# Reordering the weight conversion, the fetches and the pacing of a kernel's first 160 microseconds

## The chip, the cores and the metric

The kernel runs on one core of a Trainium2 chip. The metric is the device time of one execution in microseconds, and medians are given over repeated runs. Kernels that are compared in one experiment ran on the same chip beside runs of the kernel before, whose median there was 1023.8 to 1025.1 us.

## The reference

```python
# attention: q, k, v are (8, 8, 576, 64)
scores = q @ k.transpose(0, 1, 3, 2) / sqrt(64)
ret = scores * Dmat                   # gamma[h] ** (i - j) for i >= j, else 0
x = (ret @ v)                         # laid out as 4608 tokens of 512
# feed-forward with squared ReLU; w_in (512, 2048), w_out (2048, 512)
h = np.maximum(x @ w_in, 0.0)
out = (h * h) @ w_out
```

The weights come as 64-bit floats, and the core has to turn them into 32-bit floats itself.

## The kernel before

The work comes in three interleaved streams.

- **Retention**, 40 chunks of up to 128 tokens. TensorE makes scores, VectorE multiplies them by a mask (`ret`), TensorE transposes the next chunk's k and q (`turn`), ScalarE copies kT, and VectorE makes qT. `retain_a`, `_b` and `_c` add up the chunk's x.
- **Conversion** of w_in in 16 pieces of 128 x 512. Each piece takes five VectorE operations and two of ScalarE. `convert(n)` issues the next n parts of a list.
- **Block 0** of the feed-forward, 16 steps, one for each piece of w_in. Step j needs piece j finished. Later blocks of 28 steps follow.

Python emits everything in one order (the schedule is manual), and where the traces were read for it, ScalarE and VectorE took their share in that order: in the trace of this kernel the transposes for kT of one chunk ended at 25.95 us, and ScalarE's copy of kT began at 27.41, behind three conversion operations begun at 25.61, 26.24 and 26.80. So the place at which a part is issued among the other streams decides what it stands behind.

```python
def round_parts(j):                       # piece j; cut
    def one():
        nc.vector.tensor_scalar(exp, hi, 20, 0x7FF, ...)                 # L205
        nc.scalar.activation(exp, exp, AF.Relu, bias=..., scale=...)     # L207
    def two():
        nc.vector.tensor_scalar(bits, hi, 0xFFFFF, 0x100000, ...)        # L211
        nc.scalar.activation(frac, lo, AF.Copy, scale=2.0 ** -52)        # L212
    def three():
        nc.vector.scalar_tensor_tensor(t, bits, 2.0 ** -20, frac, ...)   # L215
    def four():
        nc.vector.tensor_tensor(t, t, exp, op=ALU.mult)                  # L218
    def five():
        nc.vector.scalar_tensor_tensor(bits, hi, 0x80000000, bits, ...)  # L221
    ...

def w_in_parts():                         # the list that convert() goes through
    end = []
    for j in range(N_W1 + 1):
        one, two, three, four, five = round_parts(j) ...
        yield from (one, two) if j < N_W1 else ()
        yield from end                    # three, four, five of piece j - 1
        ...

def first_in(j):                          # step j of block 0; cut
    assert n_made[0] > j
    for c in range(N_DM):
        nc.tensor.matmul(p, lhsT=w[:, c, :], rhs=xT[0][:, c, :], ...)    # L528, h_ps

R_0 = TOK * 3 // 2                        # tokens of retention beside block 0

def ffn(i):                               # cut: pays out steps at a rate per token
    rate = (N_W1 - 2) / R_0 if tok >= TOK else 0
    owed[0] += cs / 3 * rate
    while steps and owed[0] >= 1:
        owed[0] -= 1
        if steps[0][0] == 0:
            convert(4)
        step()

for i in range(N_CH + 1):                 # cut
    if i <= N_EARLY:                      # N_EARLY = 4
        ...retain_a, _b, _c of i - 1, with idle matmuls: warm(n)
        if i == N_EARLY: step()
        scores(i)
        warm(2)
        convert(3 if i >= 2 else 0)
        if i == N_EARLY: step()
        turn(i + 1)
        warm(1)
        convert(2 if i >= 2 else 0)
    else:
        retain_a(i - 1); convert(1); ffn(i - 1)
        retain_b(i - 1); scores(i); convert(1); ffn(i - 1)
        turn(i + 1); retain_c(i - 1); convert(1); ffn(i - 1)
    load(i + 3) ...; fetch_raw(...)       # next chunk's q, k, v; next raw pieces
```

Of the kernel before, what the change touches and what calls it, by code (L numbers as in the profile page):

```python
# [12 lines left out]
AF = mybir.ActivationFunctionType  # L13
# [4 lines left out]
TOK = 512  # L18
# [22 lines left out]
def kernel(  # L41
# [33 lines left out]
    nc = tc.nc  # L75
# [79 lines left out]
    N_W1 = N_DF  # L155
# [7 lines left out]
    def raw_of(j):  # L163
        return raw_all[j % N_RAW] if j < N_W1 else raw_all[(j - N_W1) % 3]

    def exp_of(j):
        return exp_all[j % 2] if j < N_W1 else exp_all[2 * (j % 2)]

    def piece_src(j):
        wi, m, e = pieces[j]  # L170
        f = (m + e * N_M) * 128
        if wi == 0:
            return moe_w_in.rearrange("(c p) f -> p c f", p=128)[:, :, f:f + 128]
        return moe_w_out[f:f + 128, :].rearrange("p (c f) -> p c f", c=N_DM)
# [8 lines left out]
    def as_dst(j, t):  # L183

        if pieces[j][0] == 0:
            return t.rearrange("p (c f) -> p c f", c=N_DM)
        return t.rearrange("p (o s f) -> p o s f", o=2, s=2)
# [7 lines left out]

    def round_parts(j):
        words = raw_of(j).bitcast(U32).rearrange("p (n two) -> p n two", two=2)
        lo, hi = words[:, :, 0], words[:, :, 1]
        frac = raw_of(j).rearrange("p (n two) -> p n two", two=2)[:, :, 0]
        exp = exp_of(j).bitcast(U32)  # L200
        t = piece_dst(j)
        bits = t.bitcast(U32)

        def one():
            nc.vector.tensor_scalar(exp, hi, 20, 0x7FF, op0=ALU.logical_shift_right, op1=ALU.bitwise_and)  # L205

            nc.scalar.activation(exp, exp, AF.Relu, bias=exp_bias[:, 0:1], scale=2.0 ** 23)  # L207

        def two():

            nc.vector.tensor_scalar(bits, as_dst(j, hi), 0xFFFFF, 0x100000, op0=ALU.bitwise_and, op1=ALU.bitwise_or)  # L211
            nc.scalar.activation(frac, lo, AF.Copy, scale=2.0 ** -52)  # L212

        def three():
            nc.vector.scalar_tensor_tensor(t, bits, 2.0 ** -20, as_dst(j, frac), op0=ALU.mult, op1=ALU.add)  # L215

        def four():
            nc.vector.tensor_tensor(t, t, as_dst(j, exp_of(j)), op=ALU.mult)  # L218

        def five():  # L220
            nc.vector.scalar_tensor_tensor(bits, as_dst(j, hi), 0x80000000, bits, op0=ALU.bitwise_and, op1=ALU.bitwise_or)  # L221

        if not wide:
            to = t if pieces[j][0] == 0 else t.rearrange("p o s f -> p (o s) f")
            return [lambda: nc.sync.dma_start(to, piece_src(j))] + [None] * 4
        return [one, two, three, four, five]

    def sum_w_in(mp):

# [13 lines left out]
    def w_out_parts():  # L243

        for j in range(N_W1, N_W1 + 3):
            yield lambda j=j: fetch_w(j)
        for j in range(N_W1, len(pieces)):
            *most, five = round_parts(j)
            yield from most

            def last(j=j, five=five):
                if five:
                    five()
                fetch_w(j + 3)

            yield last
            wi, m, e = pieces[j]
            mh, mq = divmod(m, N_MQ)
            if e == 1:

                at = slice(2 * mh, 2 * mh + 2)
                b = [stage[0][:, o, at, :] for o in range(4)] + [stage[1][:, o, at, :] for o in range(3)]
                r1, r2, r3, r4 = right_sums(*b)
                yield lambda r1=r1, r2=r2: (r1(), r2())
                yield lambda r3=r3, r4=r4: (r3(), r4())
            if e == 1 and mh == 1:

                for st_, at in ((stage[0], slice(0, 4)), (stage[1], slice(4, 7))):
                    yield from right_sums(*(st_[:, :, o, :] for o in range(NP)))
                    yield lambda st_=st_, at=at, mq=mq: nc.sync.dma_start(  # L270
                        w2_dram[at, :, mq, :].rearrange("o p f -> p o f"), st_.rearrange("p o s f -> p o (s f)"))
# [4 lines left out]
    def fetch_raw(count):  # L276

        for _ in range(count):
            if n_raw[0] < min(N_W1, n_made[0] + N_RAW):
                fetch_w(n_raw[0])  # L280
                n_raw[0] += 1


    def w_in_parts():

        end = []
        for j in range(N_W1 + 1):
            one, two, three, four, five = round_parts(j) if j < N_W1 else [None] * 5
            yield from (one, two) if j < N_W1 else ()
            yield from end  # L290

            def last(j=j, five=five):
                if five:
                    five()
                n_made[0] += 1
                if n_next[0]:
                    fetch_raw(2)

            end = [three, four, last]

    w_in_steps = w_in_parts()

    def convert(count):
        for _ in range(count):
            f = next(w_in_steps, None)
            f and f()
# [3 lines left out]
    exp_bias = const.tile([128, 1], F32, name="exp_bias")  # L310
    nc.gpsimd.memset(exp_bias, -896.0 * 2.0 ** 23)
    for i in range(3):
        load(i)
        fetch_raw(min(i, 1))

    ident = only.tile([128, 128], F32, name="ident")
    make_identity(nc, ident)
# [95 lines left out]
    def grown(i, h):  # L413
        nc.scalar.copy(u_sb[(2 * chunks[i][1] + h + 1) % 3], u_ps[0])
# [28 lines left out]
    def retain_c(i):  # L443

        b_, ci, c0, cs = chunks[i]
        own, grow = within(i, 0)
        more = ci + 1 < NCH
        if i < N_EARLY or i >= N_CH - 2:

            nc.scalar.copy(u_sb[(2 * ci + (cs // CH)) % 3][:, 0:2, 0:1], xp[0][:, :, cs - CH:cs - CH + 1])  # L450
        for j in range(0, len(own), 2):
            for f in own[j:j + 2] + (grow[j:j + 2] if more else []):
                f()
        if more:
            grown(i, 1)
        tok = b_ * S + c0
        at = tok
        p = xp[0][:, :, 0:256].rearrange("p a (g t) -> p a g t", g=2)
        while at < tok + cs:
            n = at // TOK  # L460

            while steps and steps[0][0] <= (n - 2 if n > 4 else n - 3):
                step()
                owed[0] -= 1
            end = min(tok + cs, (n + 1) * TOK)
            nc.scalar.copy(xT[n][:, :, at - n * TOK:end - n * TOK].rearrange("p (a g) t -> p a g t", a=2),  # L466
                           p[:, :, :, at - tok:end - tok])
            at = end
            if n_next[0] < N_BLK and (n_next[0] + 1) * TOK <= at:
                steps.extend(block_steps(n_next[0]))  # L470
                n_next[0] += 1
        st[i] = loaded[i] = None
# [154 lines left out]



    R_0 = TOK * 3 // 2  # L630
    LAG = 7

    def ffn(i):

        b, ci, c0, cs = chunks[max(0, min(i, N_CH - 1))]
        tok = b * S + c0
        if tok < TOK + R_0:
            rate = (N_W1 - 2) / R_0 if tok >= TOK else 0
        elif tok < 5 * TOK:
            rate = (3 * N_MP * NP - LAG) / (4 * TOK - TOK - R_0 + TOK)  # L640
        else:
            rate = N_MP * NP / TOK
        owed[0] += cs / 3 * rate
        while steps and owed[0] >= 1:
            owed[0] -= 1
            if steps[0][0] == 0:
                convert(4)
            step()


# [2 lines left out]
    def warm(count):  # L653
        for _ in range(count):
            nc.tensor.matmul(junk[:, 0:128], lhsT=ident, rhs=ident, start=True, stop=True)
# [4 lines left out]
    for i in range(N_CH + 1):  # L660
        if i <= N_EARLY:

            if i >= 1:
                retain_a(i - 1)
                warm(1)
                retain_b(i - 1)
                warm(1)
                retain_c(i - 1)
            if i == N_EARLY:
                step()  # L670
            scores(i)
            warm(2)
            convert(3 if i >= 2 else 0)
            if i == N_EARLY:
                step()
            turn(i + 1)
            warm(1)
            convert(2 if i >= 2 else 0)
        else:
            retain_a(i - 1)  # L680
            convert(1)
            ffn(i - 1)
            retain_b(i - 1)
            if i < N_CH:
                scores(i)
            convert(1)
            ffn(i - 1)
            if i + 1 < N_CH:
                turn(i + 1)
            retain_c(i - 1)  # L690
            convert(1)
            ffn(i - 1)
        if i + 3 < N_CH:
            load(i + 3)
        if i < N_EARLY:
            fetch_raw(1 if i < 2 else 2)
    assert n_next[0] == N_BLK
    first.close()

# [207 lines left out]
```

## Time and profile before

| | before |
|---|---|
| median of runs | 1024.22 us |
| profiled span, granted clock | 1024.3 us, 0.989 |
| TensorE idle in the whole span | 32.2 us, of it 19.3 us up to 160 us |
| step 0 of block 0 starts | 40.64 us |
| busy from 40 to 137 us | TensorE 90%, VectorE 67% |

TensorE sets the time (it is busy for 992.1 of 1024.3 us), so the reader should ask of each engine only when it makes TensorE wait. The change aims at one line of the waits of ScalarE up to 137 us (who waited <- for whom: us in total, times, longest):

```profile
ACT w L207 <- DVE w L205: 34.2, 14, 4.2
```

When L207 stood and waited for L205 in this trace, the copies of kT, u_sb and x stood behind it, and for those TensorE did wait: L207 began at 83.79 us after a wait of 3.41 us, the three copies followed at 84.90, 85.37 and 85.63, and TensorE waited 1.16 us for x, to 86.34. Its waits for u_sb are 5.9 us in all.

### The profile page before, as it was taken

Reading aid. Unit: us, or ns where it says so; the run is one execution under the profiler, and the core shown is the slowest. Engines: PE = TensorE matmul, PEld = TensorE weight load, DVE = VectorE, ACT = ScalarE, POOL = GpSimd, SP = SyncE. Lnnn points to the kernel's source line nnn. Section 1 sums busy time; section 2 is a strip of 40 time slices with the busy share of each in tenths; the row PEclk is TensorE's granted clock in tenths of the full one; section 3 lists DMA queues with packets and bytes.
Section 4 is the critical chain, followed back from the end, with each engine's and each line's share of the span. In section 5 each row is a group of like instructions: output and inputs, shape, how many; then the busy total and the mean of one; then the engine's idle time right before and its main releaser. Section 6 shows DMA issues by size and latency. Waiting matters only on the chain.

```text
span 1024.3 us, 24209 instructions
## 1 busy us (share of the span) xinstructions
PE 992.1 (97%) x10442; PEld 867.8 (85%) x10442; DVE 748.3 (73%) x1414; ACT 184.1 (18%) x425; POOL 79.6 (8%) x82
## 2 busy tenths in 40 slices
PE   7788999999999999999999999999999999999998
PEld 6444578888888888888778888999999999999997
DVE  1367858765888897898886767877777677777765
ACT  2344331121222212222221100000000000000000
POOL 1100101011011010210101000000000000000000
PEclk9899999999999999999999999999999999999999
DMA  8758556565668759769537898874855747565351
GB/s 204 192 149 232 129 150 208 144 191 166 165 232 260 219 192 288 232 184 301 185 108 280 325 414 322 310 263 170 276 200 214 275 155 252 200 240 206 124 206 42
DMA packets 187659, 220.36 MB, mean 215 GB/s; under 512 B 119200, under 2 KB 137632, under 8 KB 178592
## 3 DMA queue, kind: packets, MB, share of 16 engines
q1 hardware_dynamic: 187552, 218.81, 65.0%
q8 instruction: 82, 1.34, 0.5%
q14 instruction: 25, 0.20, 0.1%
HBM read 129.39 MB, written 89.39 MB: 214 GB/s over the span
## 4 chain that ended last, share of the span: by engine, by line
PE 87%; DVE 6%; DMA 3%; ACT 2%; SPq 1%; issue 1%; DVEq 0%; ACTq 0%
PE o_b L787 16%; PE h_b L563 15%; PE o_c L787 11%; PE o_a L787 10%; PE h_c L563 10%; PE h_a L563 10%; PE h_ps L528 5%; PE x_ps L405 3%; PE t_ps L367 2%; PE x_ps L440 2%; PE sc_ps L388 2%; DMA g_dram<-room 1%; DMA a<-g_dram 1%; PE u_ps L408 1%; DVE ret L391 1%
## 5 line engine op out<-in xcount | busy, mean ns | idle before, releaser
L563 PE MATMUL h_b<-room,w 128*128 128x256 f32 x736 | 177.6, 384 | 1.4 <-DVE room L582 1.4
L563 PEld LDWEIGHTS h_b<-room,w 128*128 128x128 f32 x736 | 136.9, 190 | 21.6 <-DVE room L582 2.2
L787 PE MATMUL o_b<-w,room 128*128 128x128 f32 x1168 | 144.5, 275 | 1.4 <-DVE room L738 1.4
L787 PEld LDWEIGHTS o_b<-w,room 128*128 128x128 f32 x1168 | 137.2, 192 | 1.6 <-DVE room L738 1.6
L787 PE MATMUL o_c<-w,room 128*128 128x128 f32 x1008 | 123.0, 275 | 0.0
L787 PEld LDWEIGHTS o_c<-w,room 128*128 128x128 f32 x1008 | 117.7, 192 | 0.0
L563 PE MATMUL h_c<-room,w 128*128 128x256 f32 x480 | 115.8, 384 | 0.0
L563 PE MATMUL h_a<-room,w 128*128 128x256 f32 x448 | 107.5, 383 | 0.0
L563 PEld LDWEIGHTS h_c<-room,w 128*128 128x128 f32 x480 | 89.3, 190 | 12.8
L563 PEld LDWEIGHTS h_a<-room,w 128*128 128x128 f32 x448 | 83.8, 190 | 12.3 <-issue 0.5
L787 PE MATMUL o_a<-w,a 128*128 128x128 f32 x688 | 85.9, 275 | 0.5 <-DMA a<-g_dram 0.5
L787 PEld LDWEIGHTS o_a<-w,a 128*128 128x128 f32 x688 | 81.3, 192 | 0.7 <-issue 0.6
L570 DVE SCALAR_TENSOR_TENSOR room<-room 128x512 f32<-128x512 f32 x96 | 70.7, 736 | 3.3
L580 POOL TENSOR_TENSOR room<-room 128x512 f32<-128x512 f32 x32 | 35.7, 1115 | 441.0 <-ACT room L579 398.0
L528 PE MATMUL h_ps<-room,w 128*128 128x512 f32 x128 | 65.2, 657 | 2.5 <-DVE w L221 1.5
L798 ACT COPY r<-o_a 128x128 f32<-128x128 f32 x54 | 14.4, 266 | 278.4 <-PE o_a L787 237.3
L375 DVE TENSOR_TENSOR qT<-t_ps,dq 128x512 f32<-128x512 f32 (+1 forms) x40 | 25.4, 634 | 44.2 <-ACT kT L373 33.7
L405 PEld LDWEIGHTS x_ps<-ret,v_ld 64*64 64x64 f32 x1152 | 40.2, 137 | 19.0 <-issue 14.5
L582 DVE TENSOR_TENSOR room<-h_b,room 128x512 f32<-128x512 f32 x32 | 22.1, 691 | 44.9 <-PE h_b L563 40.6
L405 PE MATMUL x_ps<-ret,v_ld 64*64 64x64 f32 x1152 | 50.1, 227 | 4.8 <-ACT w L466 1.6
L393 POOL TENSOR_TENSOR v_ld<-v_ld,dv 128x512 f32<-128x512 f32 (+1 forms) x40 | 43.7, 1094 | 98.0 <-DMA v_ld<-in_v_dram 91.0
L528 PEld LDWEIGHTS h_ps<-room,w 128*128 128x128 f32 x128 | 25.1, 206 | 30.7 <-issue 26.8
(95 smaller groups left out, 1364.6 us busy)
## 6 DMA issues: line engine op xcount, KB each, us to landing
g_dram<-room SPq DMA_DIRECT2D x32, 1792.0 KB, 7.2
a<-g_dram SPq DMA_DIRECT2D x43, 1024.0 KB, 6.8
room<-g_dram SPq DMA_DIRECT2D x20, 1024.0 KB, 5.9
w<-w_dram SPq DMA_DIRECT2D x7, 1792.0 KB, 11.1
out_dram<-room SPq DMA_DIRECT2D x18, 512.0 KB, 3.3
v_ld<-in_v_dram SPq DMA_DIRECT2D x32, 256.0 KB, 3.9
w<-in_moe_w_in_dram SPq DMA_DIRECT2D x16, 512.0 KB, 4.9
w<-in_moe_w_out_dram SPq DMA_DIRECT2D x16, 512.0 KB, 3.8
```

What stands on the lines that cost most here:

```text
L367: nc.tensor.transpose(p[:, h, j, hp, :], loaded[i][j][rows(h), 2 * hp:2 * hp + 2, :], ident[rows(h), rows(h)])
L375: nc.vector.tensor_tensor(to, p[:, :n_h, j, :, :], dq[:, :, c0:c0 + cs].rearrange("p d (h t) -> p h d t", h=n_h), op=ALU.mult)
L388: nc.tensor.matmul(sc[rows(h), e, hp, :], lhsT=kT[rows(e), hp, t], rhs=qT[rows(e), hp, t], start=True, stop=True, skip_group_check=True)
L393: nc.gpsimd.tensor_tensor(vs[:cs], vs[:cs], dv[:cs, :, ci:ci + 1].to_broadcast([cs, H, D]), op=ALU.mult)
L405: own.append(lambda hp=hp, e=e, b=b: nc.tensor.matmul(x_at(hp, b, h), lhsT=s["vs"][rows(h), 2 * hp + b, :], rhs=s["ret"][rows(h), e, hp, : ...
L440: nc.tensor.matmul(x_at(hp, b, h), lhsT=u[rows(e), hp, :], rhs=s["qT"][rows(e), hp, CH * h:CH * h + CH], start=clears(b, hp // 2), stop=Fa ...
L528: nc.tensor.matmul(p.rearrange("p h t -> p (h t)"), lhsT=w[:, c, :], rhs=xT[0][:, c, :], start=(c == 0), stop=(c == N_DM - 1))
L563: nc.tensor.matmul(p[:, mm, :], lhsT=w[:, c, :], rhs=xs[n][right][:, c, :], start=(j in OPENS and mm == 0 and c == 0), stop=(j in CLOSES a ...
L570: nc.vector.scalar_tensor_tensor(t, t, 0.0, t, op0=ALU.max, op1=ALU.mult)
L580: nc.gpsimd.tensor_tensor(g["A11"], g["A11"], g["A11"], op=ALU.mult)
L582: nc.vector.tensor_tensor(g["A22"], p, p15, op=ALU.add)
L787: nc.tensor.matmul(p, lhsT=s["lefts"][left][:, m, :], rhs=w_out[j][:, m, WO_SLOT[right], :], start=(i in OPENS and m == 0), stop=(i in CLO ...
```

## The change

The intent is to take ScalarE's two conversion operations out of that position and issue them one part later, when VectorE has long finished L205. The first fetches of raw pieces move, step 1 moves behind the transposes of chunk 5, and block 0 runs beside 640 tokens of retention instead of 768, so that it ends sooner. A piece now has six parts instead of five, because ScalarE's pair is a part of its own. The pieces that are converted after block 0 get a similar new order, which is cut from the diff below.

```diff
         def one():
             nc.vector.tensor_scalar(exp, hi, 20, 0x7FF, ...)
+        def two():
+            nc.vector.tensor_scalar(bits, as_dst(j, hi), 0xFFFFF, 0x100000, ...)
+        def beside():
             nc.scalar.activation(exp, exp, AF.Relu, bias=exp_bias[:, 0:1], scale=2.0 ** 23)
-        def two():
-            nc.vector.tensor_scalar(bits, as_dst(j, hi), 0xFFFFF, 0x100000, ...)
             nc.scalar.activation(frac, lo, AF.Copy, scale=2.0 ** -52)
 ...
     def w_in_parts():
 ...
+        parts = [round_parts(j) for j in range(N_W1)] + [[None] * 2]
+        yield from parts[0][0:2]
+        for j in range(N_W1):
+            beside, three, four, five = parts[j][2:]
+            yield beside
+            yield from parts[j + 1][0:2]
+            yield three
+            yield four
 ...
+            yield last
 ...
     for i in range(3):
         load(i)
-        fetch_raw(min(i, 1))
+        fetch_raw(i % 2)
 ...
-    R_0 = TOK * 3 // 2
+    R_0 = TOK * 5 // 4
 ...
             if steps[0][0] == 0:
-                convert(4)
+                convert(5)
             step()
 ...
+            convert(1 if i >= 3 else 0)
             if i == N_EARLY:
                 step()
             scores(i)
             warm(2)
-            convert(3 if i >= 2 else 0)
+            turn(i + 1)
+            warm(1)
+            convert((0, 0, 2, 5, 5)[i])
             if i == N_EARLY:
                 step()
-            turn(i + 1)
-            warm(1)
-            convert(2 if i >= 2 else 0)
 ...
         if i < N_EARLY:
-            fetch_raw(1 if i < 2 else 2)
+            fetch_raw(2 if i == 0 else 1)
```

In the changed kernel the last conversion operation is line L223 (L221 before), and the steps are L534 (L528 before).

More of the change, by code (lines that the diff above doesn't have):

```diff
@@ L205, in one @@
             nc.vector.tensor_scalar(exp, hi, 20, 0x7FF, op0=ALU.logical_shift_right, op1=ALU.bitwise_and)
-            nc.scalar.activation(exp, exp, AF.Relu, bias=exp_bias[:, 0:1], scale=2.0 ** 23)
         def two():
             nc.vector.tensor_scalar(bits, as_dst(j, hi), 0xFFFFF, 0x100000, op0=ALU.bitwise_and, op1=ALU.bitwise_or)
+        def beside():
+            nc.scalar.activation(exp, exp, AF.Relu, bias=exp_bias[:, 0:1], scale=2.0 ** 23)
             nc.scalar.activation(frac, lo, AF.Copy, scale=2.0 ** -52)
@@ L224, in round_parts @@
             to = t if pieces[j][0] == 0 else t.rearrange("p o s f -> p (o s) f")
-            return [lambda: nc.sync.dma_start(to, piece_src(j))] + [None] * 4
-        return [one, two, three, four, five]
+            return [lambda: nc.sync.dma_start(to, piece_src(j))] + [lambda: None] * 5
+        return [one, two, beside, three, four, five]
     def sum_w_in(mp):
@@ L247, in w_out_parts @@
         for j in range(N_W1, len(pieces)):
-            *most, five = round_parts(j)
-            yield from most
+            one, two, beside, three, four, five = round_parts(j)
+            yield one
+            yield lambda two=two, beside=beside: (two(), beside())
+            yield three
+            yield four
             def last(j=j, five=five):
-                if five:
-                    five()
+                five()
                 fetch_w(j + 3)
@@ L284, in w_in_parts, with last @@
     def w_in_parts():
-        end = []
-        for j in range(N_W1 + 1):
-            one, two, three, four, five = round_parts(j) if j < N_W1 else [None] * 5
-            yield from (one, two) if j < N_W1 else ()
-            yield from end
-            def last(j=j, five=five):
-                if five:
-                    five()
+        parts = [round_parts(j) for j in range(N_W1)] + [[None] * 2]
[4 more added lines that the diff above has]
+            yield from parts[j + 1][0:2]
+            yield three
+            yield four
+            def last(five=five):
+                five()
                 n_made[0] += 1
@@ L297, in last @@
                     fetch_raw(2)
-            end = [three, four, last]
+            yield last
     w_in_steps = w_in_parts()
```

## The prediction

> **What bounds the kernel now.** I read the page first, then busy time by stretches, then the list of waits of TensorE, then the timeline of the first 140 us.
>
> The page's first two sections: busy share by engine, and tenths of busy time in 40 slices of 25.6 us.
>
> ```profile
> span 1024.3 us, 24209 instructions
> PE 992.1 (97%) x10442; PEld 867.8 (85%) x10442; DVE 748.3 (73%) x1414; ACT 184.1 (18%) x425; POOL 79.6 (8%) x82
> ...
> PE   7788999999999999999999999999999999999998
> ...
> PEclk9899999999999999999999999999999999999999
> ```
>
> The reader is to see that TensorE is the bound: all of its idle time is 32 us, and the gaps I added up from the timeline put 19.3 us of that into the first 160 us. From 137 to 300 us it is busy 162.73 of 163. So TensorE's idle time at the start goes straight into the span, and so does a throttled clock. The change touches only that start: it adds no arithmetic, so it can win at most those 19 us and the throttled time.
>
> The start by stretches (start:end, their length, busy us with instruction counts for PE, PEld, DVE, ACT, POOL; granted clock; DMA share; GB/s):
>
> ```profile
> 20.00:30.00 10.00, 7.92 (x205) 6.38 (x197) 3.32 (x7) 4.59 (x10) 2.12 (x2) 0.84 0.94 220
> 30.00:40.00 10.00, 7.25 (x180) 5.94 (x180) 4.54 (x7) 3.26 (x10) 2.25 (x2) 0.84 0.94 230
> 40.00:50.00 10.00, 7.89 (x29) 3.76 (x30) 2.35 (x5) 1.18 (x4) 1.06 (x1) 0.70 0.63 166
> ...
> 60.00:70.00 10.00, 9.50 (x97) 4.34 (x95) 6.86 (x14) 3.53 (x7) 0.00 (x0) 0.85 0.68 180
> 70.00:80.00 10.00, 10.00 (x156) 5.41 (x159) 7.71 (x14) 6.48 (x13) 1.06 (x1) 1.00 0.58 184
> ```
>
> From 70 us block 0 runs with no TensorE gap although VectorE is busy 77%. That is worth explaining, because the change disturbs it. VectorE's timeline there (start, length, operation):
>
> ```profile
> 66.47 0.69 DVE L391 TENSOR_TENSOR ret<-sc_ps,msk 128x512 f32<-128x512 f32 x1 [3.00 <-PE sc_ps L388]
> 67.08 0.42 DVE L211 TENSOR_SCALAR w<-w 128x512 uint32<-128x512 uint32 x1
> 67.41 0.68 DVE L215 SCALAR_TENSOR_TENSOR w<-w,w 128x512 f32<-128x512 uint32 x1
> 68.13 0.69 DVE L218 TENSOR_TENSOR w<-w,w 128x512 f32<-128x512 f32 x1
> 68.86 0.69 DVE L221 SCALAR_TENSOR_TENSOR w<-w,w 128x512 uint32<-128x512 uint32 x1
> ```
>
> The scores end at 66.40, the mask product starts at 66.47, and piece 4 of w_in is finished at 69.55. TensorE does not wait: at 66.33 it goes on with the block-0 step of piece 3, which was finished at 62.5. The conversion is one whole piece ahead of the step that uses it. Only step 1 has no such lead, and the waits of TensorE show it as the one wait of its kind:
>
> ```profile
> PE x_ps L440 <- ACT u_sb L414: 5.9, 4, 2.2
> ...
> PE h_ps L528 <- DVE w L221: 1.5, 1, 1.5
> ```
>
> [...] a 128x512 matmul takes 592 ns as a rule and 1222 ns at most, and steps of 3.63 us took 6.32 and 5.33 us. [...] gaps of 1.33 to 2.18 us were followed by half clock five times out of six. [...] the copy kT at 27.41 stood behind three conversion steps on ScalarE. [...] here L205 took 1.28 us instead of 0.42 at 34.53, while GpSimd scaled v.
>
> **The change part by part.**
>
> Early gain. In iterations 2 and 3 ScalarE's conversion steps leave the path: kT and u_sb no longer queue behind them. The gaps of 1.44 us (to 28.85) and 2.18 us (to 37.70), both on u_sb, shrink to about 0.2 each: 3.2 us. Some 0.5 us of throttled retention goes with them. **Minus 3.7 us.** Fetching pieces 1 and 2 behind chunk 3 moves under 1 us of issue time; the pieces land 5.4 us after issue and are needed later than that. I give it zero.
>
> Old gaps that go. After 40.64 us TensorE idles 1.47, 0.59, 1.57, 0.49, 1.16, 1.75, 0.57 and 1.05 us, 8.65 in all, mostly behind kT, u_sb and copies that queue on ScalarE behind L207 waiting for L205. The new order makes ScalarE wait less. **Minus 8.6 us**, at best.
>
> The lost lead. Here I counted parts in program order. Before, 15 parts of 5 per piece are issued by the end of iteration 4, so pieces 0 and 1 are done and piece 2 is three fifths through. Afterwards it is 14 parts of 6 per piece: pieces 0 and 1 done, only two parts of piece 2. From there before issues 4 parts with a step and 3 with a chunk, afterwards 5 and 3, but over fewer tokens per step (640/14 = 46 instead of 55): 5.4 parts against 5 needed, and 6.2 against 6. So before enters each step with the next piece mostly finished, and afterwards the last part of piece j comes in the very batch before step j. The built order of both programs confirms it: each step waits for the last part of its own piece, and in the new program that part stands on VectorE behind the mask product or the qT product of the chunk whose scores or transposes stand just before the step on TensorE. This is a round trip from TensorE to VectorE and back:
> - After scores: 0.07 until ret, then start to start 0.61, 0.33, 0.72, 0.73, and 0.69 for the last, 3.15 us as in the fence, plus 0.05: 3.2 us idle. Where the second part is already done, 2.9.
> - After transposes: 0.1, kT 0.58, qT 0.61, then 0.33, 0.72, 0.73, 0.69: 3.8 us, less 0.56 of retention on TensorE: 3.2.
>
> Step by step from the new order: step 1 3.7 (one more part, less the warming matmuls), 2 3.5, 4 3.2, 5 3.2, 7 3.2, 8 2.6, 9 2.9, 10 2.4 (a half chunk), 12 2.9, 13 2.9, 15 1.5; steps 0, 3, 6, 11, 14 follow directly on another step and only the state update, and VectorE's 3.4 us fit within TensorE's 4.2. **Plus 32.0 us.**
>
> Clock. Before, the granted clock of the stretches from 40 to 137 us gives 12.8 us at half rate (6.0 + 0.4 + 3.0 + 3.4), worth 6.4 us. Afterwards gaps of 3 us come every 7 us; at a clock of about 0.85, as in the stretches at 20 to 40 us that were as full of gaps, over 110 us, 33 us would be at half rate, three quarters of them busy: 12.4. **Plus 6 us.**
>
> R_0 only moves 128 tokens of retention from beside block 0 to beside blocks 1 to 3, where TensorE is full anyway: zero.
>
> Sum: 1024.2 - 3.7 - 8.6 + 32.0 + 6 = 1049.9. I take 1048, since gaps are the part most easily overcounted.
>
> **The rivals.** First, the intent holds: the lead is not needed since VectorE has slack (77%), the steps find their weights, and the old gaps and throttled windows of the start vanish: 1024.2 - 3.7 - 8.6 - up to 6 = 1006 to 1014. For it speaks that ScalarE's wait on L205 is 34.2 us in the first 120 us; against it, that slack does not help where VectorE's queue itself stands still for TensorE (the ret product above had waited 3.00 us). Second, the round trips are there but the clock stays as it was, since steps are dense work: 1044. Third, transfers: the DMA share is 0.94 between 20 and 40 us, so earlier transposes of chunk 4 may run into its q, issued at 26.4 to 28.3 and landing about 3.6 us later; that would eat about 1 us of the early gain, no more. Fourth, the throttle holds for most of block 0: 1058.
>
> **Range and chances.** The round trips are read from a program order and durations, so I trust them to about 4 us; the clock to 6; the early gain to 2. That gives 1036 to 1058. The limit of 2% is 1044.7, under my centre but near the second rival: slower 0.62, within 2% 0.35, faster 0.03.
>
> **What would show it.** Right: TensorE's waits list h_ps <- DVE for the last conversion step about ten times and some 25 to 32 us, longest near 3.7; waits of L207 on L205 shrink from 34 us; the clock from 40 to 150 us is lower; after 160 us nothing differs. Early gain right: the first step starts near 37 us instead of 40.64. Wrong: h_ps waits on VectorE only a few times or briefly, because the pieces were finished earlier than I counted or the waits overlap gaps that I count as gone.

## The result

The changed kernel took 1062.14 us (median, 1060.49 to 1066.34) beside 1023.96 us of the kernel before. The ratio is 1.0376, with a 95% interval of 1.0332 to 1.0419: slower. Ratios here are the mean time of one kernel's fast runs over that of the other's of the same rounds, so they are not quite the ratio of the medians.

The page of the changed kernel, to be held against that of before in the prediction (the span, busy by engine, 40 slices of 26.6 us):

```profile
span 1064.6 us, 24214 instructions
PE 1009.9 (95%) x10442; PEld 875.1 (82%) x10442; DVE 746.5 (70%) x1414; ACT 185.7 (17%) x425; POOL 78.8 (7%) x82
...
PE   8677779999999999999999999999999999999998
...
PEclk9788888999999999999999999999999999999999
```

The span is 40.3 us longer. TensorE's idle time is 54.7 us instead of 32.2, so 22.5 us of the 40.3 are idle. The other 17.8 us are more busy time for the same 10442 matmuls: they ran slower. Slices 2 to 6 show the idle time and slices 2 to 7 the clock; from slice 8 on the two pages agree. TensorE's waits up to 200 us:

```profile
PE h_ps L534 <- DVE w L223: 30.7, 12, 3.7
PE u_ps L414 <- issue: 3.6, 1, 3.6
```

The steps of block 0 now wait for the last operation of their piece, twelve times, 30.7 us in all, where before it was once and 1.5 us. ScalarE's wait for L205, the target of the change, is gone from its list up to 170 us. One place where a step waits, in the timeline of VectorE; TensorE had finished the scores at 75.07:

```profile
75.14 0.69 DVE L397 TENSOR_TENSOR ret<-sc_ps,msk 128x512 f32<-128x512 f32 x1 [3.83 <-PE sc_ps L394]
75.74 0.42 DVE L209 TENSOR_SCALAR w<-w 128x512 uint32<-128x512 uint32 x1
76.08 0.69 DVE L217 SCALAR_TENSOR_TENSOR w<-w,w 128x512 f32<-128x512 uint32 x1
76.80 0.69 DVE L220 TENSOR_TENSOR w<-w,w 128x512 f32<-128x512 f32 x1
77.52 0.69 DVE L223 SCALAR_TENSOR_TENSOR w<-w,w 128x512 uint32<-128x512 uint32 x1
```

and TensorE's next piece of work there:

```profile
78.27 5.34 PE L534 MATMUL h_ps<-room,w 128*128 128x512 f32 x8 [3.20 <-DVE w L223]
```

VectorE has nothing to do for 3.83 us, because the next thing in its queue is `ret`, which needs the scores. Then it works through `ret` and four conversion operations while TensorE has nothing to do for 3.20 us. Each engine stands still while the other works. And the step that follows takes 5.34 us, where a step at full clock takes 3.70: the gap is paid for once more in the clock. The stretch of block 0 as a whole, changed kernel:

```profile
40.00:160.00 120.00, 86.99 (x796) 42.07 (x789) 56.19 (x100) 35.31 (x66) 7.39 (x7) 0.84 0.46 126
160.00:200.00 40.00, 37.85 (x458) 27.59 (x457) 26.21 (x44) 10.33 (x21) 3.09 (x3) 0.91 0.38 119
```

and the kernel before:

```profile
40.00:137.00 97.00, 87.70 (x1029) 46.12 (x1030) 64.70 (x110) 36.86 (x71) 8.10 (x7) 0.93 0.59 156
```

The granted clock is full or half (1.0 or 0.5) in every entry of the clock record in these two traces. A mean of 0.84 over 120 us is then 0.16 x 120 x 2 = 38.4 us at half rate; with the next row 45.6 us. Before it is 13.6 us. Half of the difference, 16.0 us, is the work lost, and it fits the 17.8 us of added busy time. (The trace's own record of the clock, from 40 us on, has 45.0 and 12.8 us at half rate, which gives 16.1.)

The clock record of the changed kernel has eleven stretches of half rate up to 200 us: seven of 3.41 us, three of 6.83 and one of 10.24. If this trace is cut into windows of 3.41 us at those edges, from 40 us on, all eight windows in which TensorE was busy for less than 40% were followed by half rate; of the four at 56 to 59%, two were and two were not. The length of the gap alone did not decide it: after waits of 1.47 us (1.06 us of another wait shortly before), 2.40 and 2.87 us the steps took 5.40, 6.60 and 5.40 us, but the 2.89 us of waiting before step 13 lay over two windows, 56 and 59% busy, and step 13 took 3.70 us, at full clock. So in this trace the place of a gap counted as well as its length.

### The profile page after: what moved, and what is told of

It reads as the page before. It is cut to its first block, busy times and chain, and to the rows that moved or that the text cites. A ratio compares the mean times of both kernels' runs of the same rounds, so it can differ in the third digit from the quotient of the medians.

```text
span 1064.6 us, 24214 instructions
## 1 busy us (share of the span) xinstructions
PE 1009.9 (95%) x10442; PEld 875.1 (82%) x10442; DVE 746.5 (70%) x1414; ACT 185.7 (17%) x425; POOL 78.8 (7%) x82
## 4 chain that ended last, share of the span: by engine, by line
PE 90%; DVE 6%; DMA 2%; SPq 1%; issue 1%; ACT 1%; ACTq 0%; DVEq 0%
PE h_b L569 16%; PE o_b L793 15%; PE h_c L569 11%; PE h_a L569 10%; PE o_c L793 10%; PE o_a L793 10%; PE h_ps L534 7%; PE x_ps L411 3%; PE t_ps L373 2%; PE x_ps L446 2%; PE sc_ps L394 2%; DMA a<-g_dram 1%; DVE w L220 1%; DVE w L223 1%; DVE ret L397 1%
## 5 line engine op out<-in xcount | busy, mean ns | idle before, releaser
L534 PE MATMUL h_ps<-room,w 128*128 128x512 f32 x128 | 79.6, 780 | 31.7 <-DVE w L223 30.7
L569 PEld LDWEIGHTS h_c<-room,w 128*128 128x128 f32 x480 | 89.2, 190 | 12.8
L534 PEld LDWEIGHTS h_ps<-room,w 128*128 128x128 f32 x128 | 30.5, 250 | 69.6 <-issue 35.0
L397 DVE TENSOR_TENSOR ret<-sc_ps,msk 128x512 f32<-128x512 f32 (+1 forms) x40 | 27.3, 684 | 46.9 <-PE sc_ps L394 46.9
L411 PEld LDWEIGHTS x_ps<-ret,v_ld 64*64 64x64 f32 x1152 | 40.3, 137 | 18.3 <-issue 14.2
```

The lines of the kernel that those rows point to most:

```text
L397: nc.vector.tensor_tensor(r[:cs], sc[:cs], msk[:cs].to_broadcast([cs, 2, HP, CH]), op=ALU.mult)
L411: own.append(lambda hp=hp, e=e, b=b: nc.tensor.matmul(x_at(hp, b, h), lhsT=s["vs"][rows(h), 2 * hp + b, :], rhs=s["ret"][rows(h), e, hp, : ...
L534: nc.tensor.matmul(p.rearrange("p h t -> p (h t)"), lhsT=w[:, c, :], rhs=xT[0][:, c, :], start=(c == 0), stop=(c == N_DM - 1))
L569: nc.tensor.matmul(p[:, mm, :], lhsT=w[:, c, :], rhs=xs[n][right][:, c, :], start=(j in OPENS and mm == 0 and c == 0), stop=(j in CLOSES a ...
```

## The experiments

Four questions stood after the result. Is the lost lead really the cause, and not the new order of parts as such? Is the clock a cost of its own? What became of the gain in the first 40 us? And is there a version with the gain and without the loss? Nine more kernels were run, and the changed kernel once more; all gave the right result.

### The lead given back (lead_late)

```diff
             convert((0, 0, 2, 5, 5)[i])
             if i == N_EARLY:
                 step()
+                convert(6)
```

> The changed kernel with six more conversion parts issued right after step 1, so that each later step again finds its piece finished one step earlier; everything else of the change stays. Theory (the lost lead): the waits of h_ps on the last conversion step fall from 30.7 us to 4 to 7 us (step 1 keeps its 3.7), the granted clock rises from 0.974 to 0.984 or more, and the time falls from 1062 to 1020 to 1030. Rival (the new order of the conversion's parts, the shorter R_0 or the order of fetches costs the time by itself): the time stays above 1050.

Measured: 1026.92 us (1024.01 to 1029.38), ratio to before 1.0014 (0.9979 to 1.0050), clock 0.987. TensorE's waits:

```profile
PE h_ps L534 <- DVE w L223: 5.8, 2, 4.4
PE t_ps L373 <- DVE ret L397: 5.2, 3, 3.8
```

Six parts issued earlier, once, take back 35 us. The new order, the short R_0 and the changed fetches are all still in this kernel, so none of them costs the time by itself. What remains is at the start: step 1 still waits, and its six extra parts now stand in front of chunk 5's mask product, which holds up the transposes of chunk 6 for 3.75 us.

### The lead taken from the kernel before (before_no_lead)

```diff
-            convert(2 if i >= 2 else 0)
+            convert(2 if 2 <= i < N_EARLY else 0)
         else:
+            few = 1 if i > N_EARLY + 1 else 0
...
-            convert(1)          # three times, in each chunk
+            convert(few)
```

> The kernel before with five conversion parts withheld (two at the end of iteration 4, three in iteration 5), so that it has the same zero lead as the changed kernel, with its old order of parts, its old R_0 and its old fetches. Theory (the lost lead is enough by itself): waits of h_ps on the last conversion step of 15 to 28 us instead of 1.5, a clock under 0.985, and 1042 to 1060. Rival (the lead does not matter, the new order does): 1022 to 1030.

Measured: 1057.35 us (1055.84 to 1059.29), ratio 1.0313 (1.0283 to 1.0344), clock 0.981. TensorE's waits:

```profile
PE h_ps L528 <- DVE w L221: 26.9, 12, 3.3
```

Five parts withheld from the old kernel, with nothing else touched, cost 33 us. Together with the run above this shows the lead to be the cause in both directions.

### Idle matmuls in the gaps (filled)

```diff
+    JUNK = {1: 13, 2: 11, 4: 11, 5: 11, 7: 11, 9: 10, 10: 8, 12: 10, 13: 10}
...
+        for _ in range(JUNK.get(j, 0)):
+            nc.tensor.matmul(p[:, 0, 0:128], lhsT=ident, rhs=ident, start=True, stop=True)
         for c in range(N_DM):
             nc.tensor.matmul(p, lhsT=w[:, c, :], rhs=xT[0][:, c, :], ...)
```

> The changed kernel with 8 to 13 idle matmuls of the identity (some 0.24 us each) put before nine of the steps that wait, into the PSUM tile that the step then overwrites: the round trips stay, but TensorE is busy during them. Theory (the gaps throttle the clock, and that alone costs some 16 us): the clock rises to 0.983 or more and the time falls by 8 to 14 us, to 1048 to 1054, although the steps start no earlier. Rival (the throttle has nothing to do with the gaps, or these matmuls do not hold the clock): 1060 to 1066 or more.

Measured: 1050.88 us (1049.66 to 1058.76), ratio 1.0265 (1.0219 to 1.0312), clock 0.991 (0.974 in the profile of the changed kernel). The same place as above, TensorE's timeline:

```profile
67.77 2.72 PE L535 MATMUL h_ps<-ident 128*128 128x128 f32 x22
71.48 3.70 PE L537 MATMUL h_ps<-room,w 128*128 128x512 f32 x8 [0.99 <-DVE w L223]
```

TensorE now does 2.72 us of useless work in the gap, and the step after it takes 3.70 us. Adding work made the kernel 11 us faster. The round trips themselves are all still there; what is gone is the clock's share (only step 8, which got no idle matmuls, still takes 5.40 us). So in this kernel the clock is a cost of its own, and it came with the gaps. Its size is best read inside the two profiles: from the start of step 0 to the end of step 15 the changed kernel takes 132.9 us and this one 116.2 us, 16.7 us less, close to the 16 of the theory. The medians differ by only 11 us. In this profile 3.9 us are lost again after block 0, where it has two stretches of half clock (6.8 us together) and a wait of 2.59 us for a transfer at 663 us.

### The old R_0 in the changed kernel (r0_old)

```diff
-    R_0 = TOK * 5 // 4
+    R_0 = TOK * 3 // 2
```

> The changed kernel with block 0 beside 768 tokens of retention again. Theory: the lead stays lost for most steps and is regained only slowly (6.4 parts issued for each step against 6), so the waits fall from 30.7 to 18 to 27 us and the time to 1045 to 1058. Rival (the shorter R_0 was the cause): the waits are under 8 us and the time under 1032.

Measured: 1049.98 us (1048.14 to 1052.73), ratio 1.0245 (1.0227 to 1.0264). The steps still wait for L223 ten times, 24.6 us in all; from 105 us on the gaps shrink to 1.1 to 2.2 us. With more retention for each step more parts are issued for each step, and the lead grows back slowly. R_0 decides how fast a lost lead returns, not whether it is lost.

### The short R_0 in the kernel before (before_r0)

```diff
-    R_0 = TOK * 3 // 2
+    R_0 = TOK * 5 // 4
```

> The kernel before with block 0 beside 640 tokens of retention alone. Theory: its lead of a whole piece is kept (5.2 parts issued for each step against 5 needed), so the waits on the last conversion step stay at 1.5 us and the time within 4 us of before, 1020 to 1028. Rival (VectorE has too little slack for the denser steps): h_ps waits 5 us or more on it and the time is over 1030.

Measured: 1020.69 us (1019.69 to 1023.87), ratio 0.9971 (0.9951 to 0.9990). The waits of h_ps on L221 are one of 2.2 us. The denser block 0 is harmless as long as the lead is there, and may be worth 3 us.

### The old order of fetches (fetch_old)

```diff
-        fetch_raw(i % 2)
+        fetch_raw(min(i, 1))
...
-            fetch_raw(2 if i == 0 else 1)
+            fetch_raw(1 if i < 2 else 2)
```

> The changed kernel with the first fetches of w_in's pieces as before. Theory (the gap of 3.61 us at 28.1 us, which waits for nothing that the profile shows, comes from the two pieces fetched together in front of chunk 4): the gap is gone, the first step of block 0 starts at 37 to 38.5 us instead of 41.7, and the time falls by 4 to 6 us. Rival (the gap is a supply of instructions that TensorE reaches too early in any order): a gap of 2 us or more without a releaser remains near 28 us and the time stays within 2 us of 1062.

Measured: 1061.22 us (1058.51 to 1064.33), ratio 1.0341 (1.0304 to 1.0379). The gap without a releaser is still there, 1.70 us long, and ends at 31.18 us; step 0 starts at 40.34 us. This is between the two expectations: the gap is shorter, but the time stays. The order of the two fetches is not what took the early gain.

### The changed kernel once more (after_again)

No edit; a second profile, with one run.

> The changed kernel unchanged, for a second profile. If the 3.61 us without a releaser at 28.1 us belongs to the supply of instructions in that one execution (lead_late and filled have the same program up to there and show no such gap), it is absent or of another size here and step 0 starts at 37 to 39 us; if it belongs to the change, it is there again with 3 us or more. The waits of h_ps on the last conversion step are 29 to 32 us either way.

Measured: 1066.75 us in the single run. The waits on L223 are again 30.7 us in twelve, and single gaps agree with the first profile's to 0.02 us. Near 28 us there is no gap without a releaser, which is the first of the two outcomes, though step 0 starts at 39.48 us, a little later than expected. In place of the gap the transposes of chunk 4 wait:

```profile
32.03 0.76 PE L373 MATMUL t_ps<-ident,k_ld 64*128 64x64 f32 x4 [2.24 <-DMA k_ld<-in_k_dram]
```

Here a reader can see why one profile is not enough for a gap of 3 us. The cause named changes from one profile to the next, but the standstill ends at 31.72, 32.03, 31.18 (fetch_old) and 31.43 us (r0_old). The DMA packets in the packed traces point to what TensorE lacked in the first profile. The page of the changed kernel lists a queue of instructions (packets, MB, share):

```profile
q8 instruction: 82, 1.34, 0.5%
```

There are 82 packets of 16 KB, and 21058 records of TensorE's matmuls, weight loads and sequencer in that trace, some 257 to a packet. In the traces of the kernel before and of the changed kernel's first profile, TensorE has three waits of over 0.3 us without a releaser in the first 50 us: 0.49 us (to 23.99) before, 0.67 us (to 22.99) and 3.61 us (to 31.72) in the changed kernel. They stand after 706, 706 and 962 of these records, and they end 1.51, 1.32 and 1.44 us after such a packet has landed (at 22.48, 21.67 and 30.28 us). That the 3.61 us were a wait for TensorE's own instructions is read from these three waits and is not shown by an experiment; the 2.24 us here were a wait for k of chunk 4.

### The lead restored where VectorE stands idle (lead_early)

```diff
-            convert(1 if i >= 3 else 0)
+            convert((0, 0, 0, 1, 6)[i])
...
-            convert((0, 0, 2, 5, 5)[i])
+            convert((0, 0, 2, 5, 6)[i])
```

> The changed kernel with the lead restored where VectorE stands idle: six parts instead of one ahead of step 0 in iteration 4 and six instead of five after the transposes, so that piece 1 is finished ahead of the mask product of chunk 4 and piece 2 ahead of step 1. Theory (lead): the waits of h_ps on the last conversion step fall under 2 us, the 4.44 us before step 1 and the 3.75 us before the transposes of chunk 6 in lead_late go, and the time is 1014 to 1021, faster than the kernel before by 0.3 to 1%. Rival (the waits at the start only move to the next wait, on ScalarE or a transfer): 1022 to 1028, as lead_late.

Measured: 1016.07 us (1015.00 to 1016.78), ratio 0.9919 (0.9907 to 0.9932), clock 0.989. No wait of h_ps on VectorE is left in TensorE's list; its largest waits up to 170 us are:

```profile
PE t_ps L373 <- DVE ret L397: 2.5, 4, 1.2
PE u_ps L414 <- issue: 2.2, 1, 2.2
```

Placed ahead of step 0, the parts run on VectorE while it would wait for chunk 4's scores. This version beats both kernels. The interval shows it faster than before by 0.7 to 0.9%, though that is inside the 2% that counts as the same.

### Raw pieces behind chunk 4 (fetch_late)

```diff
 (on top of lead_early)
-            fetch_raw(2 if i == 0 else 1)
+            fetch_raw((0, 3, 1, 1)[i])
```

> lead_early with pieces 1 and 2 (and 3) fetched only behind chunk 4's loads. In the profiles of the changed order TensorE stands still until 30.7 to 32.0 us either for k of chunk 4 or, in the middle of a run of matmuls, for nothing that the profile shows. Theory (the transfers cap the early gain: 1 MB of w_in in front of chunk 4 takes some 4.6 us at the 220 GB/s of that stretch): the standstill near 28 to 32 us falls under 1 us, step 0 starts at 37 to 39 us, and the time is 1 to 3 us under lead_early. Rival (the supply of instructions or the loads themselves cap it whatever is in front): a standstill of 1.5 us or more is still there and the time is within 1 us of lead_early or above.

Measured: 1014.06 us (1012.46 to 1015.62), ratio 0.9892 (0.9872 to 0.9912). The standstill near 28 to 32 us is gone: no gap of 0.4 us or more is left between 17 and 35 us. Step 0 starts at 37.87 us instead of 40.69. But it now waits for VectorE, whose conversion has moved back with the fetch:

```profile
PE h_ps L534 <- DVE w L223: 2.8, 1, 2.8
```

and VectorE's timeline ahead of it:

```profile
34.90 0.43 DVE L205 TENSOR_SCALAR w<-w 128x512 uint32<-128x512 uint32 x1 [2.20 <-DMA w<-in_moe_w_in_dram]
```

This is what the theory expects. But it is one profile against one, and lead_late and filled, which have these transfers in front of chunk 4, started step 0 at 38.93 and 37.57 us. That the transfers cap the early gain is therefore likely but not shown. The next limit in this profile is the last three parts of piece 0, which stand on VectorE behind the first part of piece 1, and that waits 2.20 us for its fetch. Step 0 is 2.8 us earlier; the time is 2 us shorter, but the two kernels ran in different calls and their intervals touch, so no gain over lead_early is shown.

### Step 0 behind the scores (step_behind)

```diff
 (on top of lead_early)
-            if i == N_EARLY:
-                step()
             scores(i)
-            warm(2)
+            if i == N_EARLY:
+                step()
+            else:
+                warm(2)
```

> lead_early with step 0 behind the scores of chunk 4, so that the copy of x that it waits for (1.04 us in every profile) lies beside the scores, and the mask product beside step 0. Theory: the wait of 1.04 us goes and step 0 takes the place of the warming matmuls (0.7 us): 1 to 2 us under lead_early, 1014 to 1015.5. Rival (the wait moves to the scores, which need the copy's neighbours on ScalarE or the transposes' qT): within 0.5 us of lead_early.

Measured: 1014.06 us, but spread from 1009.14 to 1019.91; ratio 0.9885 (0.9849 to 0.9921). The wait of step 0 on the copy of x fell from 1.04 to 0.45 us, while the transposes of chunks 5 and 6 wait 0.99 and 1.49 us for `ret` (in lead_early those of chunk 6 waited 0.82 us and those of chunk 5 under 0.5). The gain against lead_early is inside the spread: inconclusive.

## Why the prediction was right or wrong

The direction and the cause were right; the size was wrong. 1062.14 us lies outside the stated range of 1036 to 1058, and the mechanism gave 38 us instead of 24.

**The lost lead: right.** The term was plus 32.0 us; the waits measured 30.7. The list by step holds one by one: predicted 3.7, 3.5, 3.2, 3.2, 3.2 for steps 1, 2, 4, 5 and 7, and measured 3.71, 3.24, 3.20, 3.22 and 3.20. The largest error was step 8, 2.6 predicted and 1.47 measured, since a wait of 1.06 us on ScalarE came first. This part came from counting parts in program order and reading five durations from the trace, and lead_late and before_no_lead show it to be causal.

**The clock: the step that failed.** The prediction wrote "Plus 6 us". The measured busy time grew by 17.8 us. Two factors of that term were wrong. First, the length: it took 110 us at 0.85, 33 us at half rate; measured were 0.84 over 120 us and 0.91 over 40 more, 45.6 us at half rate. The mean clock itself was estimated well, but not how long it lasted, because the slow steps stretched the phase itself: block 0 took 132.9 us, and 95.2 before. Second, the factor: it took "three quarters of them busy". The half-rate time did not fall on gaps and work alike. It came after the gap, on the next step: ten of the twelve steps behind a gap on L223 took 5.34 to 6.7 us (13 and 14 ran at full clock), and those that follow another step directly 3.70. So nearly all of the half-rate time was working time, worth 22.8 us instead of 12.4; less the 6.8 us of before (half of 13.6), that is 16.0 instead of 6. filled confirms it from the other side: with the gaps filled, block 0 is 16.7 us shorter in the profile, and the median 11 us.

**The early gain: failed.** "Minus 3.7 us" came out as zero. The waits on u_sb did go. Yet step 0 started at 41.74 and 39.48 us in the two profiles of the changed kernel, and at 40.64 us before; over all profiles that leave step 0 in its place, it started between 37.6 and 41.7 us with the new order and the changed kernel's fetches (six profiles) and between 39.0 and 40.6 us with the old order and fetches (three). The prediction's third rival saw that transfers could eat the gain, but put it at "about 1 us" and at q; in fact TensorE stood still for k of chunk 4 in one profile (2.24 us) and, as the packets suggest, for its own instructions in another (3.61 us). That these came late because of the w_in transfers in front of chunk 4 is likely, but fetch_late alone does not show it.

**The old gaps: too high, and the cause is not shown.** "Minus 8.6 us, at best" measured minus 5.4: after step 0, the gaps other than those on L223 sum to 3.3 us (8.65 before). Of the 8.65 us, 5.0 were waits on ScalarE and 1.47 was step 1's wait for VectorE. The waits on ScalarE fell to 1.6 us, and in lead_early they are 1.6 too. But before_r0, which keeps ScalarE's operations in their old place, also has only 1.6 us of them. So the shorter R_0 is enough for that fall, and no run moves ScalarE's pair alone. What its new place is worth stays open; the waits on u_sb before step 0 did go, but the standstill near 30 us took their place. Part of lead_early's gain of 8 us is the short R_0 as well, which alone was worth 3 us.

**R_0: right only while the lead is there.** By itself it is worth little (before_r0, minus 3 us). With the lead lost it decides how fast the lead returns: the old R_0 takes the ratio from 1.0376 to 1.0245 (r0_old), some 13 us. The prediction has this inside its count of parts and not in its term for R_0.

Taken together: 30.7 - 5.4 + 16.0 + 0 = 41.3, against the 40.3 us by which the profiled spans differ; since step 0 started 1.1 us later in this profile, the sum is good to about 2 us only. Of the rivals the fourth, 1058, came nearest by its number, but not by its reason: the clock was at half rate for 44 of the 133 us of block 0, not for most of it.

Two smaller slips in the prediction did not decide the outcome. It reads "no TensorE gap" from 70 us on, which holds to 80 us; later gaps of 1.16, 1.75, 0.57 and 1.05 us stand in its own list. And its tolerances of 4, 6 and 2 us, added, give 1060 as the upper end and not 1058.

## What to carry to other kernels

When a producer's parts are issued in batches between a consumer's steps, count in program order how far ahead each part is of its use; here a lead of zero turned twelve of sixteen steps into round trips between TensorE and VectorE, 30.7 us of waiting, and the busy shares of the kernel before (TensorE 90%, VectorE 67%) did not show it coming. Price a gap on TensorE with the clock: here a gap of about 3 us cost, in most cases, another 1.7 us in the step behind it (5.34 to 5.40 us instead of 3.70), half as much again. And before booking a gain from a removed wait, ask what arrives next at that place.
